# Message passing over 640,000 edges: buckets in pairs that share 33 tiles, and overflow worked off in batches

## The chip, the cores and the metric

The kernel runs on one core of one Trainium2 chip. The time is the device time of one execution in microseconds (us). Before the change the median of three runs is 8543.91 us (8543.35 to 8546.97); the execution that the profile shows took 8539.33 us. Engines are PE (TensorE), DVE (VectorE), ACT (ScalarE), POOL (GpSimd) and SP (SyncE); PEld is the weight load of PE.

## What is computed

```python
N, deg, C, L, DE = 10000, 64, 64, 1, 4        # E = 640,000 edges, M = 4
R = _silu(edge_feat @ w_rad)                              # (E, C)
xs = x[src]                                                 # (E, C, M)
tp = jnp.einsum('eci,ef,ifo->eco', xs, Y, cg)             # (E, C, M)
msg = R[:, :, None] * tp
agg = _segment_sum(msg.reshape(-1, C * M), dst, N).reshape(N, C, M)
return jnp.einsum('ncm,cd->ndm', agg, w_mix)
```

`src` and `dst` are random. So each edge needs a row of `x` (256 numbers, 1 KB) picked by its `src`, and its message has to be added to the node `dst`.

## The kernel before

Edges are sorted by `dst` in two passes and then summed per bucket of 32 nodes (`NB`). There are 313 buckets; 18 of them are a group (`B`), and there are 18 groups, the last with 7 buckets. A **tile** is 128 edges, one per partition. An edge is carried as 9 words: a key (`src` and `dst`), four of `Y`, four of `edge_feat`.

- The edges are cut into three parts by `SPLIT`; a bucket has 5, 6 and 6 tiles (`BT`, 17 in all) for them in a DRAM tensor `bkt`. What a part doesn't hold goes on into the tiles of the next one, and what all 17 don't hold goes to an overflow region behind the buckets.
- `pass1` sorts a part into groups (DRAM tensor `grp`), `pass2` a group into its buckets. Both work in **chunks** of 12 tiles through `route`: one-hot matrices by DVE and ACT (`spread` L578, `rows` L594 and L600), matmuls that put the edges into rows (L608), and one indirect store per chunk from POOL (L619). For every batch of chunks `tables` computes where rows go, in a chain of some 50 small DVE instructions with PE and ACT in between.
- `messages` goes over **units**, one per bucket and part (939). A unit gathers the rows of `x` by one indirect DMA from POOL per tile (L915, five units ahead, into seven buffers), evaluates the radial weights (L933 to L949), multiplies (L967), spreads `Y` over the 32 nodes (`spots`, L957 and L960) and sums on PE (L980). Sums of parts 0 and 1 go to DRAM and are added in the next part (L1009); in the last part four buckets at a time are mixed and written to the output (L1028, L1036).
- Order. PE, DVE and ACT follow the order in which the generators are called. First `pass1` of part 0 runs alone. Then `groups` steps through the first segment of `pass2`, with steps of `pass1` of part 1 between, until the first bucket data are there. After that each unit takes four steps; beside the units of a part run `pass2` of the same part (next group) and `pass1` of the next part, paced by `ends` and `later`. Beside the units of the last part only `pass2` runs. POOL and SP get their instructions in the same program order and work them off in that order.
- After the last unit, `overflow` (L1142) loops over the overflow regions of `grp` and `bkt`, one tile of 128 edges a turn: load, gather `x`, match equal destinations, multiply, read the output rows, add, write them back. `whole` (L1172) would redo everything if a chunk had needed more than 128 rows.

The row capacity of a bucket and its layout are set by two lines:

```python
self.p2 = Pass(12, 15, BT * P // 15, 6, True)      # rows of 15 edges, 145 rows in 17 tiles
nc.vector.tensor_tensor(dl[:N], cap[:N], off[:N], op=OP.min)
```

Of the kernel before, what the change touches and what calls it, by code (L numbers as in the profile page):

```python
# [25 lines left out]
P = 128  # L26
# [7 lines left out]
BT = 17  # L34
UT = 6
SPLIT = ((0.3, (5,)), (0.355, (6,)), (0.345, (6,)))
# [4 lines left out]
FAR = 2097152.0  # L41
KR = 108
HB = 5
# [30 lines left out]
class Kernel:  # L74
    def __init__(self, ctx, tc, x, src, dst, Y, ef, w_rad, cg, w_mix, out):
# [17 lines left out]
        assert N <= 1 << 14 and BT == sum(sum(u) for _, u in SPLIT)  # L93
# [15 lines left out]
        self.p2 = Pass(12, 15, BT * P // 15, 6, True)  # L109
# [3 lines left out]
        self.NBK = (N + NB - 1) // NB  # L113

        self.btile = [0]
        for _, u in SPLIT:
            self.btile.append(self.btile[-1] + sum(u))

        self.p1.ovf = len(SPLIT) * NG * self.p1.stride
        self.p2.ovf = self.NBK * self.p2.stride  # L120
        for q, tiles in ((self.p1, [z - a for a, z in self.part]), (self.p2, sum(self.gt, []))):
            q.none = -(-(q.ovf + sum((t + q.T - 1) // q.T for t in tiles) * P + 16) // q.stride) * q.stride
            q.rows = q.none
# [20 lines left out]
    def consts(self):  # L144
# [8 lines left out]
        self.zr = c.tile([16, max(self.p1.rw, self.p2.rw)], F, name="zr")  # L153
        nc.vector.memset(self.zr, 0.0)
        self.pid = iota("pid", [[0, 1]], cm=1)
        self.pid1 = iota("pid1", [[0, 1]], base=1, cm=1)
# [60 lines left out]
        self.bb = iota("bb", [[self.p2.stride, B]])  # L217
# [23 lines left out]
    def bucket_words(self, b, n, t0, t1):  # L241

        v = self.p2.dst[:self.p2.ovf, :].rearrange("(b s) w -> b (s w)", s=self.p2.stride)
        return v[b:b + n, t0 * P * W:t1 * P * W].rearrange("b (p q) -> p b q", p=P)

    def clear_buckets(self):
        nc, n = self.nc, 2048 // (BT * W)
        for b in range(0, self.NBK, n):
            m = min(n, self.NBK - b)
            nc.sync.dma_start(self.bucket_words(b, m, 0, BT),  # L250
                              self.z[:, :m * BT * W].rearrange("p (b q) -> p b q", b=m))
            yield
# [100 lines left out]
    def tables(self, ps, D, nt, rows, kov, base, cap):  # L353
# [36 lines left out]
        nc.tensor.matmul(pre_p[:N, 32:32 + B], self.ones[0:1, :N], rows, start=True, stop=True)  # L390
        nc.tensor.matmul(pre_p[0:1, 64:64 + B], self.ones[:N, 0:1], cn[:N], start=True, stop=True)
# [3 lines left out]
        nc.scalar.activation(off[:N], pre_p[:N, 32:32 + B], AF.Copy)  # L395
        nc.scalar.activation(tot[0:1], pre_p[0:1, 64:64 + B], AF.Copy)
        self.held = None
        yield
        if ps.carry:
# [7 lines left out]
            nc.vector.tensor_tensor(off[:N], off[:N], f[:N], op=OP.add)  # L407
            self.floor(tot[0:1], tot[0:1], r, True, ps.key, 1)
# [25 lines left out]
        nc.vector.tensor_tensor(dl[:N], cap[:N], off[:N], op=OP.min)  # L434
        nc.vector.tensor_tensor(dl[:N], dl[:N], base[:N], op=OP.add)
# [39 lines left out]
        nc.tensor.matmul(dd_p[:, :N * J], self.ones[:N, :], bd[:N, :N * J], start=True, stop=True)  # L475
        yield
        nc.vector.scalar_tensor_tensor(sts[:, :N * J], sts[:, :N * J], self.pid, dd_p[:, :N * J],
# [6 lines left out]
        di = w("di", NC, d=I32)  # L484
        nc.vector.tensor_copy(di[:, :N], dest[:, :N])
        nc.vector.tensor_scalar(di[:, :N], di[:, :N], ps.stride - 1, None, op0=OP.bitwise_and)
        nc.vector.tensor_scalar(fl[:, :N], di[:, :N], float(ps.cap), None, op0=OP.is_ge)
# [269 lines left out]
    def pass2(self):  # L757
# [13 lines left out]
        def front(i, Wt):  # L771
# [4 lines left out]
            nc.vector.tensor_scalar(base, self.bb, float(g * B * ps.stride), None, op0=OP.add)  # L776
# [11 lines left out]
            yield from self.tables(ps, D, nt, kc, self.kov[:, 1:2], base, self.bc)  # L788
            ready[i] = D, Wt, self.tab[ps.key]

        for i, (k, g) in enumerate(self.segs):
# [27 lines left out]
            n = sum(SPLIT[k][1])  # L819
# [18 lines left out]
    def messages(self):  # L838
# [19 lines left out]
        def index(k):  # L858

            g, j, s = units[k]  # L860
            if s or j:
                return
# [471 lines left out]
```

## Time and profile before

| | us | note |
|---|---|---|
| median of three runs | 8543.91 | |
| profiled execution | 8539.33 | its span, first to last instruction: 8537.6 |
| until the first gather of `x` | 614.0 | `pass1` of part 0 and the first segment of `pass2` |
| gathers of `x` and what runs beside them | 614 to 8449 | 5321 gathers, one per tile |
| after the last gather | 88 | last unit, three turns of the overflow loop |

The page gives each engine's busy time. Matmuls are pipelined and their ends are modelled, so PE's share reads high. A gather or store from POOL counts as busy while POOL prepares it; the time until its data have landed isn't in that number. A row of the windows view gives, for a stretch of time, each engine's busy time with the number of its instructions in brackets, then the clock granted to PE, the mean busy share of the DMA engines, and GB/s.

### The profile page before, as it was taken

To read this page: it belongs to the slowest core of one execution; us is meant where nothing else is said; L and a number is where in the kernel's file an instruction comes from. 1 tells how busy PE (TensorE), PEld (TensorE's weight loads), DVE (VectorE), ACT (ScalarE), POOL (GpSimd) and SP (SyncE) were. 2 spreads that over 40 slices of the span, in tenths; PEclk is the share of its full clock that TensorE was granted. 3 is DMA by queue.
4 is the path that set the end of the run, shared out by engine and by line. 5 is a ranking of instruction groups with operands and counts; after the bars stand their busy time and mean duration, and the time that the engine had idled before them with its cause. 6 is when DMAs were issued, how large, how long until landed. Compare 5 with 4: busy or idle time off the path is not lost. (4 is left out here: it accounts for less than half of the span.)

```text
span 8537.6 us, 148817 instructions
## 1 busy us (share of the span) xinstructions
PE 6849.6 (80%) x51885; PEld 6294.3 (74%) x51885; DVE 6833.0 (80%) x12901; ACT 4467.9 (52%) x12655; POOL 5984.1 (70%) x6255
## 2 busy tenths in 40 slices
PE   7977888888888788787787888876888878787875
PEld 6867777777778677777777777766777777677764
DVE  8988898889898789888888988876767767676743
ACT  6866666666566465555555655533433434343421
POOL 2236777677677767777777777777777777777774
PEclk9989999999899899899998998988888988898887
DMA  8313444344334434444444444444444444444442
GB/s 177 101 58 98 121 118 125 108 122 118 113 116 124 124 112 138 130 135 136 132 135 136 134 135 134 131 140 130 130 125 128 127 126 127 125 126 124 127 124 80
DMA packets 694591, 1056.58 MB, mean 124 GB/s; under 512 B 250979, under 2 KB 498340, under 8 KB 693840
## 3 DMA queue, kind: packets, MB, share of 16 engines
q0 software_dynamic: 284864, 746.68, 30.0%
q1 hardware_dynamic: 406384, 292.76, 12.3%
q8 instruction: 410, 6.72, 0.3%
q10 hardware_dynamic: 2592, 7.63, 0.3%
q14 instruction: 341, 2.79, 0.1%
HBM read 856.08 MB, written 203.45 MB: 124 GB/s over the span
## 5 line engine op out<-in xcount | busy, mean ns | idle before, releaser
L915 POOL DMA_INDIRECT xg<-in_x_dram,sidx x5321 | 5062.2, 951 | 1709.2 <-issue 1386.7
L608 PE MATMUL pr<-X,oh 128*128 128x135 f32 (+1 forms) x21112 | 2783.1, 291 | 400.2 <-ACT rt L615 256.8
L608 PEld LDWEIGHTS pr<-X,oh 128*128 128x128 f32 x21112 | 2662.8, 203 | 481.3 <-ACT rt L615 315.1
L980 PE MATMUL G<-S,xg 128*128 128x128 f32 x21284 | 2872.2, 296 | 155.5 <-DVE Gp L1009 116.7
L980 PEld LDWEIGHTS G<-S,xg 128*128 128x128 f32 x21284 | 2723.8, 210 | 198.7 <-DVE Gp L1009 142.9
L967 DVE TENSOR_TENSOR xg<-xg,pre 128x1536 f32<-128x1536 f32 (+1 forms) x939 | 1559.0, 1660 | 918.0 <-DMA xg<-in_x_dram,sidx 701.7
L600 ACT ACTIVATE sq<-i,rowf 128x128 f32<-128x128 f32 x6106 | 1876.1, 392 | 5.6 <-DVE rowf L565 2.4
L578 DVE TENSOR_TENSOR X<-dv,Wt 128x1512 f32<-128x1512 f32 (+3 forms) x905 | 1579.7, 1746 | 147.0 <-PE pr L608 100.0
L949 ACT ACTIVATE pre<-pre 128x384 f32<-128x384 f32 (+1 forms) x939 | 430.4, 458 | 1391.4 <-PE pre L946 1099.4
L601 ACT ACTIVATE oh<-sq,ones 128x896 f32<-128x896 f32 (+2 forms) x905 | 964.3, 1066 | 28.8 <-issue 1.4
L960 DVE TENSOR_TENSOR S<-dv,pay 128x768 f32<-128x768 f32 (+1 forms) x939 | 857.5, 913 | 64.3 <-PE G L980 20.1
L619 POOL DMA_INDIRECT grp<-rt,idx x417 | 418.6, 1004 | 573.8 <-ACT rt L615 244.9
L594 DVE TENSOR_TENSOR oh<-dv,rowf 128x640 f32<-128x640 f32 (+2 forms) x870 | 719.3, 831 | 0.5
L933 PE MATMUL pre<-identb,e 128*108 128x128 bf16 x1878 | 273.7, 229 | 500.6 <-DVE xg L967 492.9
L933 PEld LDWEIGHTS <-e 128*108 128x108 bf16 x1878 | 219.7, 132 | 572.1 <-issue 505.8
L619 POOL DMA_INDIRECT bkt<-rt,idx x488 | 488.6, 1001 | 192.5 <-issue 111.2
L938 ACT ACTIVATE sT<-pre 108x256 bf16<-108x256 f32 x939 | 351.5, 374 | 424.6 <-PE pre L933 423.2
L1028 PE MATMUL po<-wf,Gs 128*128 128x256 f32 (+2 forms) x1392 | 401.4, 453 | 160.0 <-DVE Gs L1009 158.8
L1028 PEld LDWEIGHTS po<-wf,Gs 128*128 128x128 f32 (+2 forms) x1392 | 289.8, 214 | 251.2 <-DVE Gs L1009 164.6
L896 ACT ACTIVATE e<-er 128x360 bf16<-128x360 f32 (+3 forms) x420 | 188.9, 450 | 416.1 <-DVE er L906 415.5
L615 ACT ACTIVATE rt<-pr 128x135 f32<-128x135 f32 (+1 forms) x905 | 242.5, 272 | 286.3 <-DMA bkt<-rt,idx 213.9
L548 ACT ACTIVATE pc<-pp 128x432 f32<-128x432 f32 (+4 forms) x453 | 233.5, 515 | 254.2 <-DVE pos L557 131.9
(247 smaller groups left out, 5257.3 us busy)
## 6 DMA issues: line engine op xcount, KB each, us to landing
xg<-in_x_dram,sidx POOLq DMA_INDIRECT x5321
sums<-Gp SPq DMA_DIRECT2D x626, 128.0 KB
old<-sums SPq DMA_DIRECT2D x626, 128.0 KB
bkt<-z SPq DMA_DIRECT2D x24, 994.5 KB
pay<-bkt SPq DMA_DIRECT2D x34, 486.0 KB
ys<-in_Y_dram SPq DMA_DIRECT2D x104, 96.0 KB
es<-in_edge_feat_dram SPq DMA_DIRECT2D x104, 96.0 KB
out_dram<-ot SPq DMA_DIRECT2D x69, 128.0 KB
```

The costliest lines, as they stand in the source:

```text
L578: nc.vector.tensor_tensor(X[:, :m, :].rearrange("p t (s w) -> p t s w", w=W), msk.unsqueeze(3).to_broadcast([P, m, ps.r, W]), QD[c // Q][1 ...
L594: nc.vector.tensor_tensor(oh[:, :v, :], self.v128.unsqueeze(1).to_broadcast([P, v, P]), row[:, o:o + v].unsqueeze(2).to_broadcast([P, v, P ...
L600: nc.scalar.activation(sq[:, u, :], self.i128, AF.Square, bias=to, scale=-1.0)
L601: nc.scalar.activation(oh[:, v:v + len(at), :], sq[:, :len(at), :], AF.Relu, bias=self.ones[:, 0:1], scale=-2.0)
L608: nc.tensor.matmul(pr[:, :ps.rw], oh[:, u, :], X[:, u, :], start=(u == 0), stop=(not on and u == m - 1))
L619: st = nc.gpsimd.indirect_dma_start(out=ps.dst, out_offset=bass.IndirectOffsetOnAxis(ap=idx[:, i:i + 1], axis=0), in_=RT.pop(c), in_offset ...
L915: nc.gpsimd.indirect_dma_start(out=xg[:, t, :], out_offset=None, in_=self.x, in_offset=bass.IndirectOffsetOnAxis(ap=si[:, u:u + 1], axis=0))
L933: nc.tensor.matmul(pre[:KR, 256 + 128 * h:384 + 128 * h], e[:, 36 * t:36 * t + KR], self.identb, start=True, stop=True)
L960: nc.vector.tensor_tensor(S[:, :ut], self.eq[:, :ut].unsqueeze(3).to_broadcast([P, ut, NB, 4]), pb[:, :, 1:5].unsqueeze(2).to_broadcast([P ...
L967: nc.vector.tensor_tensor(V, V, R.unsqueeze(3).to_broadcast([P, ut, 64, 4]), op=OP.mult)
L980: nc.tensor.matmul(G[:, h].rearrange("p n f -> p (n f)"), V[:, t, 32 * h:32 * h + 32, :].rearrange("p c i -> p (c i)"), S[:, t].rearrange( ...
L1028: nc.tensor.matmul(po[:nn, :256], Gs[:, h, f].rearrange("p b n -> p (b n)")[:, :nn], self.wf[:, h, f, :], start=(h + f == 0), stop=(h + f ...
```

## The change

**Pairs.** Buckets 2m and 2m+1 get 33 tiles together (`PT`). The even one fills them from the front, the odd one from the back; in parts 0 and 1 each has its own 5 and 6 tiles, and in the last part the even one has 6, the odd one 5, and the sixth tile of the even one belongs to both. So a pair of units in the last part gathers 11 tiles and not 12. The even unit builds a second spread matrix (`Sx`) for the shared tile with the odd bucket's nodes, and the odd unit adds it to its sum with the tile's products kept from the even unit. `tables` works out the row offsets from both ends; in the last part it also works out a row limit per bucket (`dlim`, `lm`), since the border between the two is free.

**Shares.** The parts now hold 0.32, 0.37 and 0.31 of the edges (before 0.30, 0.355 and 0.345). `pass1` has 134, 154 and 129 chunks (before 124, 148, 145), `pass2` 157, 175 and 157 (before 140, 174, 174).

**Overflow.** Counting the edges of the reference's inputs through these rules gives 19 overflow rows of 15 before (285 slots, three tiles) and 60 rows now (900 slots, eight tiles). Up to eight tiles (`LT`) are taken as two batches of four (`batch`, `join`, `put`): gathered and multiplied in steps beside the last units, and read, added and written back after them. Whatever remains, `grp` overflow and `whole` are put into one loop (`rest`), which isn't entered when all counts are zero.

**Pacing.** `pass1` of part 1 starts with step 40 of the units (`at`), and no longer beside the first segment of `pass2`. The blocks of the radial casts are 4 buckets (`HB`, before 5).

```diff
-SPLIT = ((0.3, (5,)), (0.355, (6,)), (0.345, (6,)))
+SPLIT = ((0.32, 5), (0.37, 6), (0.31, 6))
-HB = 5
+HB = 4
-        self.p2 = Pass(12, 15, BT * P // 15, 6, True)
+        self.p2 = Pass(12, 15, PT * P // 15, 6, True)
...
+            nc.vector.tensor_tensor(end[:H], off[:H], tot[:H], op=OP.add)
+            till = of(end, 1)
+            if final:
+                lim, dlim = w("lim", B), w("dlim", J)
+                till = w("till", B // 2)[:H]
+                nc.vector.tensor_scalar(till, of(end, 1), float(self.most_odd), None, op0=OP.min)
...
+            nc.vector.scalar_tensor_tensor(of(sh, 1), till, -1.0, of(off, 1), op0=OP.mult, op1=OP.subtract)
+            nc.vector.tensor_tensor(off[:H], off[:H], f[:H], op=OP.add)
+            nc.vector.scalar_tensor_tensor(of(off, 1), of(sh, 1), float(self.full), of(off, 1), op0=OP.add, op1=OP.add)
...
-            nc.sync.dma_start(pay[:, :nb, :], self.bucket_words(g * B, nb, self.btile[k], self.btile[k + 1]))
+            if k == len(SPLIT) - 1:
+                q = 2 * n - 1
+                v = pay[:, :a * q].rearrange("p (b t) w -> p b (t w)", t=q)
+                for u, z in ((0, n - 1), (n - 1, n), (n, q)):
+                    nc.sync.dma_start(v[:, :, u * W:z * W], self.pair_words(m, a, t0 + u, t0 + z))
+            else:
+                v = pay[:, :B * n].rearrange("p (b a t) w -> p b a (t w)", a=2, t=n)
+                nc.sync.dma_start(v[:, :a, 0], self.pair_words(m, a, t0, t1))
+                nc.sync.dma_start(v[:, :nb // 2, 1], self.pair_words(m, nb // 2, PT - t1, PT - t0))
...
+        def place(g, j):
+            n = SPLIT[g[0]][1]
+            if g[0] < FIN:
+                return j * n, n
+            return j // 2 * (2 * n - 1) + j % 2 * n, n - j % 2
...
+            if shared(k):
+                eq = ph.tile([P, NB], F, name="eqx", bufs=1)
+                nc.vector.tensor_scalar(eq, self.v128[:, NB:2 * NB], dl[:, ut - 1:ut], None, op0=OP.is_equal)
+                S = SX[k + 1] = ph.tile([P, NB, 4], F, name="Sx")
+                nc.vector.tensor_tensor(S, eq.unsqueeze(2).to_broadcast([P, NB, 4]),
+                                        pb[:, ut - 1, 1:5].unsqueeze(1).to_broadcast([P, NB, 4]), op=OP.mult)
...
+            terms = [(V[:, t], S[:, t]) for t in range(ut)]
+            if k in VX:
+                terms.append((VX.pop(k), SX.pop(k)))
...
-        later, at = [], 0
+        later, at = [], 40
...
         while segs[0] not in self.pay:
             next(sort)
-            if later:
-                said = next(later[0][0])
-                done += 0.0 if said == "held" else said or 1
+        batch, got = self.batch(), None
...
+            elif got is None:
+                if segs[-1] in self.pay:
+                    run(sort)
+                    self.remains()
+                    got = "begun"
+            elif got != "ready":
+                got = next(batch) or got
             next(main)
         assert not later
-        run(main)
-        run(sort)
+        for _ in main:
+            if got != "ready":
+                got = next(batch) or got
+        while got != "ready":
+            got = next(batch) or got
+        run(batch)
...
+    def put(self, al, di, xg):
+        nc = self.nc
+        cur = al("ocur", [P, OT, 256])
+        nc.vector.memset(cur, 0.0)
+        for t in range(OT):
+            nc.gpsimd.indirect_dma_start(
+                out=cur[:, t], out_offset=None, in_=self.out, in_offset=bass.IndirectOffsetOnAxis(ap=di[:, t:t + 1], axis=0),
+                bounds_check=self.N - 1, oob_is_err=False)
+        for t in range(OT):
+            nc.vector.tensor_tensor(cur[:, t], cur[:, t], xg[:, t].rearrange("p c i -> p (c i)"), op=OP.add)
+            nc.gpsimd.indirect_dma_start(
+                out=self.out, out_offset=bass.IndirectOffsetOnAxis(ap=di[:, t:t + 1], axis=0), in_=cur[:, t], in_offset=None,
+                bounds_check=self.N - 1, oob_is_err=False)
...
+    def rest(self):
+        with self.tc.For_i(0, self.nc.values_load(self.n[:, 3:4], min_val=0, max_val=1), 1):
+            wx = self.ph.tile([P, 2, 64, 4], F, name="wx")
+            self.wide(wx)
+            self.leftover(self.p1, self.kov[:, 0:1], self.n[:, 0:1], 0, wx)
+            self.leftover(self.p2, self.kov[:, 1:2], self.n[:, 1:2], LT * P, wx)
+            self.whole(self.n[:, 2:3], wx)
```

The order on POOL shows three places where the change moves work. `grp` and `bkt` rows are stores of the two sort passes, `xg` rows the gathers; a count behind a row stands for that many alike in a row. First the last group segments of the last part, before:

```order
L915 DMA xg<-in_x_dram,sidx 128x256 x54
L619 DMA bkt<-rt,idx 223232x135 x2
L915 DMA xg<-in_x_dram,sidx 128x256 x12
L619 DMA bkt<-rt,idx 223232x135
L915 DMA xg<-in_x_dram,sidx 128x256 x6
L619 DMA bkt<-rt,idx 223232x135
L915 DMA xg<-in_x_dram,sidx 128x256 x6
```

and the same place now:

```order
L990 DMA xg<-in_x_dram,sidx 128x256 x55
L673 DMA bkt<-rt,idx 143360x135
L990 DMA xg<-in_x_dram,sidx 128x256 x11
L673 DMA bkt<-rt,idx 143360x135 x2
L990 DMA xg<-in_x_dram,sidx 128x256 x11
L673 DMA bkt<-rt,idx 143360x135 x2
```

Two units gathered 12 tiles between stores and now gather 11; the density of stores per unit stays one. Counted over the whole order, POOL issues 5321 gathers before and 5165 now, and 905 and 906 sort stores.

Second, the change from the first pass to the units, before:

```order
L619 DMA grp<-rt,idx 165888x126 x126
L619 DMA bkt<-rt,idx 223232x135
L619 DMA grp<-rt,idx 165888x126 x2
L619 DMA bkt<-rt,idx 223232x135 x3
L915 DMA xg<-in_x_dram,sidx 128x256 x35
```

and now:

```order
L673 DMA grp<-rt,idx 165888x126 x134
L673 DMA bkt<-rt,idx 143360x135 x4
L990 DMA xg<-in_x_dram,sidx 128x256 x9
L673 DMA bkt<-rt,idx 143360x135
L990 DMA xg<-in_x_dram,sidx 128x256 x7
```

All 134 stores of part 0 stand ahead, and the four stores that `pass1` of part 1 had there (126 + 2 less 124) have moved behind the first gathers. Between the first and the last gather of part 0 there are now 329 sort stores (before 303), of part 1 295 (before 310), of part 2 144 (before 160).

Third, the end of the program, now:

```order
L1220 DMA oxg<-in_x_dram,osm 128x256 x8
L990 DMA xg<-in_x_dram,sidx 128x256 x162
L1300 DMA ocur<-out_dram,osm 128x256 x4
L1305 DMA out_dram<-ocur,osm 10000x256 x4
L1300 DMA ocur<-out_dram,osm 128x256 x4
L1305 DMA out_dram<-ocur,osm 10000x256 x4
```

The eight gathers of the batches stand 162 gathers ahead of the end; the reads and writes of the output follow the last gather in two rounds of four.

More of the change, by code (lines that the diff above doesn't have):

```diff
@@ L858, in index, with shared @@
+        def shared(k):
+            g, j = units[k]
+            return g[0] == FIN and j % 2 == 0 and j + 1 < self.nb(g[1])
         def index(k):
[L860 to L861 removed]
+            g, j = units[k]
+            if j:
                 return
             m = self.nb(g[1])
[L864 to L866 removed]
```

502 lines of the change are left out of this document (299 added, 203 removed).

## The prediction

> **What bounds the kernel now.** I read the busy times first, then the stretches of the program in the windows view, then POOL's own waits, and last the timeline of the end.
>
> ```profile
> PE 6849.6 (80%) x51885; PEld 6294.3 (74%) x51885; DVE 6833.0 (80%) x12901; ACT 4467.9 (52%) x12655; POOL 5984.1 (70%) x6255
> ```
>
> By this row PE and DVE look like the bound and POOL like the third. POOL's timeline says otherwise (columns: start, duration, engine, line, operation, count, idle time before it):
>
> ```profile
> 6932.87 1.00 POOL L619 DMA_INDIRECT bkt<-rt,idx  x1 [0.30 <-issue]
> 6934.18 1.00 POOL L619 DMA_INDIRECT bkt<-rt,idx  x1 [0.30 <-issue]
> ...
> 8445.82 0.95 POOL L915 DMA_INDIRECT xg<-in_x_dram,sidx  x1 [0.30 <-issue]
> 8447.07 0.95 POOL L915 DMA_INDIRECT xg<-in_x_dram,sidx  x1 [0.30 <-issue]
> 8448.32 0.95 POOL L915 DMA_INDIRECT xg<-in_x_dram,sidx  x1 [0.30 <-issue]
> ```
>
> Each gather is busy for 0.95 us and 0.30 us follow in which POOL waits for nothing shown: a gather takes a slot of 1.25 us, a store 1.31. So a POOL that shows 76% busy is full. The windows, cut at the first gather (614) and at the last gathers of the three parts (3085 and 5866, found by counting 1565 and 1878 gathers; 8450):
>
> ```profile
> 614.00:3085.00 2471.00, 2020.31 (x15952) 1882.77 (x15953) 2132.39 (x4131) 1534.33 (x4451) 1779.05 (x1852) 0.92 0.40 116
> 3085.00:5866.00 2781.00, 2236.03 (x17532) 2083.05 (x17531) 2385.12 (x4380) 1517.28 (x4243) 2100.14 (x2190) 0.91 0.46 134
> 5866.00:8450.00 2584.00, 2063.22 (x14548) 1871.92 (x14547) 1745.80 (x2987) 949.85 (x2578) 1957.84 (x2054) 0.87 0.43 126
> ```
>
> The columns after the length are PE, PEld, DVE, ACT and POOL. POOL's slots: 1852 x 1.25 = 2315 us of 2471 (94%), 2190 x 1.25 = 2738 of 2781 (98%), 2054 x 1.25 = 2568 of 2584 (99%). **The second and third stretches last as long as POOL needs to issue its indirect DMAs.** The first one leaves 156 us over, at DVE 86% and PE 82%. There POOL does wait for others:
>
> ```profile
> POOL xg L915 <- PE G L980: 50.8, 29, 6.9
> POOL bkt L619 <- ACT rt L615: 17.5, 10, 8.2
> ```
>
> It waits for a gather buffer that PE hasn't summed yet, or for rows that are not ready: DVE, PE and ACT are late in a burst of sorting, and the gathers have run out of buffers.
>
> **The change part by part**
>
> *Slots of POOL.* By the order of the change: gathers 5321 to 5165, batch gathers 0 to 8; sort stores behind the first gather, part by part, 303 to 329, 310 to 295, 160 to 144. The slots change by +26, -15 and -156 - 16 + 8 = -164, at 1.25 us: **+33, -19, -205 us**. All of it is on the path in the second and third stretches, which are full; in the first only if POOL stays the bound.
>
> *The first part* gets more sorting per unit: 26 chunks more, since 157 + 154 chunks replace 140 + 148, and since those that ran before the first gather have moved in here. The price of a chunk for DVE comes from a stretch of the first part:
>
> ```profile
> 800.00:2800.00 2000.00, 1670.07 (x13342) 1561.66 (x13341) 1752.08 (x3272) 1282.36 (x3724) 1465.82 (x1526) 0.93 0.41 118
> ...
> L578 DVE TENSOR_TENSOR X<-dv,Wt 128x1512 f32<-128x1512 f32 (+2 forms) x254 | 451.1, 1776 | 71.8 <-PE pr L608 56.3 <-DVE dv L575 0.5
> L967 DVE TENSOR_TENSOR xg<-xg,pre 128x1280 f32<-128x1280 f32 x256 | 379.3, 1481 | 82.4 <-ACT pre L949 65.1 <-DMA xg<-in_x_dram,sidx 15.6
> L960 DVE TENSOR_TENSOR S<-dv,pay 128x640 f32<-128x640 f32 x256 | 211.1, 825 | 30.3 <-PE G L980 11.5
> L957 DVE TENSOR_TENSOR dv<-dv,dlc 128x160 f32<-128x160 f32 x256 | 85.0, 332 | 5.1
> L906 DVE TENSOR_TENSOR er<-pay,e 128x100 f32<-128x100 f32 (+1 forms) x57 | 14.2, 249 | 0.0
> L906 DVE TENSOR_TENSOR er<-er,e 128x100 f32<-128x100 f32 (+1 forms) x57 | 14.2, 249 | 0.0
> ...
> L403 DVE SCALAR_TENSOR_TENSOR part<-f,pre 64x18 f32<-64x18 f32 x54 | 9.3, 172 | 1.8
> ```
>
> 256 units and 254 chunks ran in these 2000 us. The units' own DVE work is 379 + 211 + 85 + 28 = 704 us; the rest, 1752 - 704 = 1048, is sorting: 4.13 us a chunk. 26 chunks are 107 us. `tables` gets five more small instructions like the last row (18 tables x 5 x 0.17 = 15 us) and the radial casts a fifth block per group (5 us): DVE's 2132 us become 2259. If POOL stayed the bound the part would grow by 33 us; at the share of DVE that the whole part shows (86.3%) by 2259 / 0.863 - 2471 = 147. I take 88.0%, just above the 87.6% of the stretch quoted, because the second part runs at 86% with POOL full and bursts are what hurts: 2259 / 0.88 = 2567, **+96 us**, ends +33 and +147.
>
> *The second part* has 15 chunks less and stays with POOL: **-19 us**. Its own table instructions (20 us) lie under POOL's 2719.
>
> *The last part.* POOL falls to (2054 - 164) x 1.25 = 2363 us plus the 16 left over: 2379. Is something else late then? DVE has 1746 us; less 16 chunks (66) and the shorter odd units (a tile's share of L967 and L960 above: 156 x 0.46 = 72), plus the second spread matrix (156 pairs, two instructions), the tables and the batches. For the 128 x 128 product of the pair the nearest row is
>
> ```profile
> L1220 DVE TENSOR_TENSOR odup<-oeq,L x3: 291/291/292, 8478.7 to 8519.2; 128x128 f32<-128x128 f32 x3
> ```
>
> so 0.29 us and some 0.2 for the 32 columns: 156 x 0.5 = 78. Tables and batches I put at 60. DVE ends near 1746, 73%: cover enough. PE's matmuls for the sums stay (the odd unit has 5 + 1 terms). A chunk costs PE
>
> ```profile
> L608 PE MATMUL pr<-X,oh 128*128 128x135 f32 (+1 forms) x21112 | 2783.1, 291 | 400.2 <-ACT rt L615 256.8
> ```
>
> 2783 / 905 = 3.1 us and some smaller matmuls, say 3.4. So 2063 - 54 (16 chunks) + 30 for the batches (two times 52 matmuls at 0.29) = 2039 us, 86% of 2379. That is more than any part shows on average, but a sorting burst before has had
>
> ```profile
> 6880.00:6960.00 80.00, 74.11 (x589) 69.82 (x590) 72.17 (x137) 47.80 (x133) 60.57 (x64) 0.98 0.44 130
> 6960.00:7030.00 70.00, 47.93 (x301) 41.28 (x300) 35.08 (x54) 12.91 (x36) 52.94 (x57) 0.78 0.43 123
> ```
>
> PE at 93% with POOL at its 64 slots in 80 us, and 68% in the calm behind it. Gathers run up to five units ahead, so a burst in which PE falls back by a few us is made up in the next calm. I add 10 us for that: **-195 us**, ends -205 and -29 (below). Bucket data come in three DMAs a segment where one was; each is an SP instruction of 0.38 us, and there is slack:
>
> ```profile
> L822 SPq DMA_DIRECT2D pay<-bkt x54: 378/384/384, 606.8 to 8202.8; - x54
> ...
> L867 DVE TENSOR_SCALAR sidx<-pay x54: 183/247/439, 613.6 to 8265.8; 128x108 int32<-128x108 int32 x34, 128x90 int32<-128x90 int32 x17, 128x42 int32<-128x42 int32 x2, 128x35 int32<-128x35 int32 x1
> ```
>
> the last load was issued 63 us before its first reader ran. The batches' gathers add a wait on DVE: the product of the batch stands some two units behind the gather in DVE's order, and POOL comes to that gather only after those of five units. Behind it wait the products of the next units, and PE; POOL goes on, since its next five units have buffers. That is part of the 10 us.
>
> *Until the first gather.* Ten more chunks of `pass1`, while the first segment loses the chunks of part 1 that ran beside it:
>
> ```profile
> 200.00:300.00 100.00, 47.63 (x28) 1.00 0.40 107
> 400.00:500.00 100.00, 52.93 (x31) 1.00 0.25 85
> 520.00:614.00 94.00, 20.12 (x12) 0.70 0.08 24
> ```
>
> These are the products L578, one a chunk: 3.2 to 3.6 us a chunk, so +34. Of the 12 chunks in the last 94 us, 8 belong to part 1, with a table; without them DVE has some 40 us less of its 72 in that stretch, but the chain of the segment's own table stays. I take -34, net **0**, ends -15 and +25.
>
> *After the last gather.* Before:
>
> ```profile
> 8464.77 0.48 SPq L1037 DMA_DIRECT2D out_dram<-ot  x1
> 8475.37 40.78 SPq L1159 DMA_DIRECT2D opay<-bkt  x3
> ...
> 8489.33 1.02 POOL L1264 DMA_INDIRECT out_dram<-ocur,odi  x1 [8.18 <-DVE ocur L1263]
> 8512.16 1.03 POOL L1264 DMA_INDIRECT out_dram<-ocur,odi  x1 [8.17 <-DVE ocur L1263]
> 8530.33 1.03 POOL L1264 DMA_INDIRECT out_dram<-ocur,odi  x1 [8.68 <-DVE ocur L1263]
> ...
> 8533.94 0.14 DVE L1180 TENSOR_SCALAR nw<-cw 1x1 int32<-1x1 f32 x1 [3.90 <-PE cw L1178]
> ```
>
> From 8449.3 to the span's end at 8537.6 are 88 us: 17 until the last output is written, 64 for the loops with three turns of 18 to 23 us, the rest for the last check. Now the 17 stay; two rounds follow, each of four reads (5 us), landing and adding (3), four writes partly beside it and their landing (4): 24 us; then one check, some 6 us. That is 47: **-40 us**, ends -50 and -20.
>
> Sum: 0 + 96 - 19 - 195 - 40 = -158. Against the profiled execution's 8539.3 that is 8381; the median of the runs is 4.6 us above it, so I forecast **8385 us**.
>
> [...] A gather's busy time hardly varies:
>
> ```profile
> L915 POOL DMA_INDIRECT xg<-in_x_dram,sidx x5321: 940/946/1440, 614.0 to 8448.3; - x198
> ```
>
> The median is 946 ns and the longest of 5321 is 1440, with DVE busy beside them. [...]
>
> **The rivals**
>
> 1. *The first part stays with POOL.* For it: gathers have five units of room. Against it: DVE would stand at 2259 of 2504, 90%, above any long stretch here. Then +33 in place of +96: 8322 us.
> 2. *PE becomes the bound of the last part*, and the saved gathers show only in part. If PE can't pass the 82% of the first part: 2039 / 0.82 = 2487, -97 in place of -195: 8482. If it can't pass its present 80%, the part takes 2555, -29, and the sum is +8: no change. For it: bursts at 93%. Against it: the calm between them.
> 3. *Slower: the first part's sorting chain blocks the units.* A table is a chain through DVE, PE and ACT, each in order; when units and chunks come more densely, each hold-up of DVE delays products, sums, and so buffers. DVE's share would have to fall under 2259 / (2471 + 96 + 158) = 83% for the whole to be slower; at 80% the part takes 2824, +353, and the time is 8640. Against it: more work ready on an engine tends to raise its share.
> [...]
> 5. *The overflow isn't covered*: the count of rows would be wrong, or the last loop is entered, and the end costs what it did, or 40 us more: 8425 to 8465. The same count gives the three turns seen before.
>
> **How the numbers follow.** Forecast with its ends in the sum (8340 to 8440) 0.53; rival 1: 0.15; rival 2: 0.16, a quarter of it at no change; rival 3: 0.06; rivals 4 and 5: 0.05 each. A measurement of this kernel tells about 0.2% (17 us) from no change. Faster by more: 0.90; within it: 0.04; slower: 0.06. The range reaches down over rival 1 (8295) and up past most of rival 2 (8500).
>
> **What would show it.** In the changed profile, gathers of the last part follow each other at 1.25 us and the part lasts near 2380 us (rival 2: nearer 2490, with POOL waiting for L980's successor). The first part lasts near 2570 and shows DVE at 88%. [...] I am wrong if the last part's length doesn't follow POOL's slots, or if the first part gives back over 150 us.

## The result and the profile after

The changed kernel takes 8447.18 us (median of 4 runs, 8445.14 to 8450.74) beside 8545.39 us of the kernel before on the same chip (4 runs, 8543.35 to 8546.97): ratio 0.9885, interval 0.987 to 0.9899. It is 98 us faster; the forecast was 158. The profiled execution has a span of 8449.0 us.

The first row of its page, busy times by engine:

```profile
PE 6864.1 (81%) x52108; PEld 6331.2 (75%) x52108; DVE 6900.6 (82%) x13656; ACT 4481.6 (53%) x12845; POOL 5851.5 (69%) x6113
```

POOL fell from 70% to 69% of a shorter span and is still the least conspicuous of the three. The stretches tell more. First a correction of my own: the bounds that the prediction set for the stretches (3085 and 5866) stood some 20 us ahead of the last gathers of their parts. Divided at the end of the 1565th, 3443rd and last gather, the kernel before reads, in the windows view (columns as in the prediction: PE, PEld, DVE, ACT, POOL, granted clock, DMA), with POOL's gathers of the first stretch alone in the last row:

```profile
614.00:3105.70 2491.70, 2038.12 (x16105) 1899.19 (x16106) 2149.69 (x4159) 1552.06 (x4503) 1794.87 (x1868) 0.92 0.40 117
3105.70:5885.10 2779.40, 2234.23 (x17500) 2081.60 (x17499) 2386.32 (x4387) 1512.86 (x4225) 2098.85 (x2189) 0.91 0.46 134
5885.10:8449.30 2564.20, 2046.50 (x14423) 1856.26 (x14423) 1727.29 (x2953) 936.54 (x2542) 1943.31 (x2039) 0.87 0.43 126
8449.30:8537.60 88.30, 28.69 (x114) 20.15 (x113) 25.19 (x104) 3.61 (x14) 10.95 (x12) 0.60 0.05 13
...
614.00:3105.70 2491.70, 1491.27 (x1565) 0.92 0.40 117
```

and the changed kernel, divided at the same gathers:

```profile
603.30:3263.80 2660.50, 2168.89 (x16794) 2020.34 (x16793) 2262.58 (x4516) 1666.32 (x4866) 1820.40 (x1894) 0.90 0.39 110
3263.80:6015.40 2751.60, 2227.67 (x17244) 2082.02 (x17243) 2356.91 (x4391) 1473.13 (x4141) 2084.14 (x2173) 0.90 0.47 135
6015.40:8377.80 2362.40, 1951.92 (x14208) 1781.02 (x14206) 1726.04 (x3461) 874.93 (x2456) 1791.45 (x1875) 0.91 0.45 128
8377.80:8449.00 71.20, 12.65 (x65) 9.79 (x63) 7.91 (x14) 0.76 (x2) 16.03 (x17) 0.63 0.07 20
```

Each stretch less its counterpart, beside the forecast's term:

| stretch | before, us | after, us | change | forecast |
|---|---|---|---|---|
| until the first gather | 614.0 | 603.3 | -11 | 0 |
| first part | 2491.7 | 2660.5 | +169 | +96 |
| second part | 2779.4 | 2751.6 | -28 | -19 |
| last part | 2564.2 | 2362.4 | -202 | -195 |
| after the last gather | 88.3 | 71.2 | -17 | -40 |
| sum | 8537.6 | 8449.0 | -89 | -158 |

The last part goes by POOL's slots: 1875 instructions at 1.25 us are 2344 of its 2362 us, as 2039 were 2549 of 2564 before, and PE's share rose from 80% to 83% without ending it. The surprise is the first part. Its DVE work is what was forecast (2259; here 2263 us), but DVE's share *fell* from 86.3% to 85.0%. Where it idles is in the groups by line. DVE's product that spreads the payload into X, before the change and after it, in that part:

```profile
L578 DVE TENSOR_TENSOR X<-dv,Wt 128x1512 f32<-128x1512 f32 (+2 forms) x305 | 542.2, 1778 | 76.3 <-PE pr L608 57.0 <-DVE dv L575 0.9
```

```profile
L632 DVE TENSOR_TENSOR X<-dv,Wt 128x1620 f32<-128x1620 f32 (+2 forms) x334 | 584.2, 1749 | 151.4 <-PE pr L662 129.4 <-PE pre L1016 0.5
```

X has three buffers, and one comes free when PE's matmuls `pr` have read it. The wait for that grew by 72 us. That this is about the 73 us by which the part overran its forecast proves nothing by itself: DVE's idle time in the part grew by 56 us in all.

The end of the changed kernel, POOL's timeline from the last gather on (start, duration, engine, line, operation, count, idle time before it):

```profile
8376.89 0.95 POOL L990 DMA_INDIRECT xg<-in_x_dram,sidx  x1 [0.30 <-issue]
8399.10 1.02 POOL L1300 DMA_INDIRECT ocur<-out_dram,osm  x1 [21.26 <-issue]
...
8406.96 1.02 POOL L1305 DMA_INDIRECT out_dram<-ocur,osm  x1 [2.94 <-DVE ocur L1304]
8410.03 1.00 POOL L1305 DMA_INDIRECT out_dram<-ocur,osm  x1 [2.05 <-issue]
8413.06 0.97 POOL L1305 DMA_INDIRECT out_dram<-ocur,osm  x1 [2.02 <-issue]
8416.05 0.97 POOL L1305 DMA_INDIRECT out_dram<-ocur,osm  x1 [2.02 <-issue]
8419.12 1.04 POOL L1300 DMA_INDIRECT ocur<-out_dram,osm  x1 [2.10 <-DMA out_dram<-ocur,osm]
...
8430.22 1.00 POOL L1305 DMA_INDIRECT out_dram<-ocur,osm  x1 [2.58 <-DMA out_dram<-ocur,osm]
8433.22 0.97 POOL L1305 DMA_INDIRECT out_dram<-ocur,osm  x1 [2.00 <-DMA out_dram<-ocur,osm]
8436.21 0.97 POOL L1305 DMA_INDIRECT out_dram<-ocur,osm  x1 [2.02 <-DMA out_dram<-ocur,osm]
```

The four writes of a batch stand 3.0 us apart, not 1.3. In the second batch the profile names what each waits for, the landing of the write ahead; in the first it names nothing ("issue"), and an experiment below decides.

### The profile page after: what moved, and what is told of

Read it like the earlier page. It is cut to its first block, busy times and chain, and to the rows that moved or that the text cites. A ratio compares the mean times of both kernels' runs of the same rounds, so it can differ in the third digit from the quotient of the medians.

```text
span 8449.0 us, 149894 instructions
## 1 busy us (share of the span) xinstructions
PE 6864.1 (81%) x52108; PEld 6331.2 (75%) x52108; DVE 6900.6 (82%) x13656; ACT 4481.6 (53%) x12845; POOL 5851.5 (69%) x6113
## 5 line engine op out<-in xcount | busy, mean ns | idle before, releaser
L990 POOL DMA_INDIRECT xg<-in_x_dram,sidx x5165 | 4918.3, 952 | 1783.0 <-issue 1357.6
L662 PE MATMUL pr<-X,oh 128*128 128x126 f32 (+1 forms) x21146 | 2810.6, 293 | 460.7 <-ACT rt L669 318.9
L1056 PE MATMUL G<-S,xg 128*128 128x128 f32 x20660 | 2794.8, 297 | 86.2 <-DVE Gp L1079 63.0
L1056 PEld LDWEIGHTS G<-S,xg 128*128 128x128 f32 x20660 | 2645.6, 210 | 127.8 <-DVE Gp L1079 87.7
L1043 DVE TENSOR_TENSOR xg<-xg,pre 128x1536 f32<-128x1536 f32 (+1 forms) x939 | 1517.2, 1616 | 654.8 <-DMA xg<-in_x_dram,sidx 425.6
L632 DVE TENSOR_TENSOR X<-dv,Wt 128x1620 f32<-128x1620 f32 (+4 forms) x906 | 1582.4, 1747 | 210.2 <-PE pr L662 163.2
L655 ACT ACTIVATE oh<-sq,ones 128x1024 f32<-128x1024 f32 (+3 forms) x906 | 967.4, 1068 | 29.8 <-PE pr L662 1.6
L1029 DVE TENSOR_TENSOR S<-dv,pay 128x768 f32<-128x768 f32 (+1 forms) x939 | 836.7, 891 | 50.7 <-PE G L1056 5.8
L971 ACT ACTIVATE e<-er 128x240 bf16<-128x240 f32 (+6 forms) x522 | 205.3, 393 | 330.5 <-DVE er L981 308.9
L602 ACT ACTIVATE pc<-pp 128x432 f32<-128x432 f32 (+3 forms) x471 | 236.7, 503 | 240.9 <-DVE pos L611 128.7
L1026 DVE TENSOR_TENSOR dv<-dv,dlc 128x192 f32<-128x192 f32 (+1 forms) x939 | 325.4, 347 | 15.8
```

The source lines that it names most:

```text
L632: nc.vector.tensor_tensor(X[:, :m, :].rearrange("p t (s w) -> p t s w", w=W), msk.unsqueeze(3).to_broadcast([P, m, ps.r, W]), QD[c // Q][1 ...
L655: nc.scalar.activation(oh[:, v:v + len(at), :], sq[:, :len(at), :], AF.Relu, bias=self.ones[:, 0:1], scale=-2.0)
L662: nc.tensor.matmul(pr[:, :ps.rw], oh[:, u, :], X[:, u, :], start=(u == 0), stop=(not on and u == m - 1))
L990: nc.gpsimd.indirect_dma_start(out=xg[:, t, :], out_offset=None, in_=self.x, in_offset=bass.IndirectOffsetOnAxis(ap=si[:, u:u + 1], axis=0))
L1029: nc.vector.tensor_tensor(S[:, :ut], self.eq[:, :ut].unsqueeze(3).to_broadcast([P, ut, NB, 4]), pb[:, :, 1:5].unsqueeze(2).to_broadcast([P ...
L1043: nc.vector.tensor_tensor(V, V, R.unsqueeze(3).to_broadcast([P, ut, 64, 4]), op=OP.mult)
```

## The experiments

My theory A for the first part: the new shares put more sorting chunks beside the same units, and a chunk costs more than its DVE time. Rival B: the pairing itself costs it (longer tables, blocks of four buckets for the radial casts, two loads a segment). Rival C: the pacing, which no longer runs the next part's sorting beside the first segment.

**Four kernels on a slower chip.** The shares alone in the kernel before:

```diff
-SPLIT = ((0.3, (5,)), (0.355, (6,)), (0.345, (6,)))
+SPLIT = ((0.32, (5,)), (0.37, (6,)), (0.31, (6,)))
```

> The kernel before with the shares 0.32, 0.37, 0.31 of the edges and nothing else of the change: 18 sort chunks more for the buckets of the first part's first pass, 4 more of the second; 325 stores in the first part instead of 303, 10 more ahead of it, gathers 5321 as before. Theory A (the first part lost its 182 us because more chunks stand beside the same units, at some 7 us a chunk where I had reckoned 4.1): first part 2471 + 22 x 7 = 2625 us (2590 to 2650), first gather 15 to 35 us later than before (614), last part shorter by its 16 stores, 20 us, end as before: 8620 to 8680 us in all. Rival B (the loss comes from the pairing: longer tables, blocks of four buckets for the radial casts, two loads): first part 2471 to 2520 us, 8500 to 8570 in all. Rival C (the pacing of the part's sorting ahead of the next part): like B, first part under 2520.

The changed kernel with the pacing of before; the third kernel has the same with three steps of `later` beside each step of `sort`:

```diff
-        later, at = [], 40
+        later, at = [], 0
...
         while segs[0] not in self.pay:
             next(sort)
+            said = next(later[0][0])
+            done += 0.0 if said == "held" else said or 1
```

> The changed kernel with the pacing of before: the sorting of the next part runs from the first quarter on and beside the first segment ahead of the first gather (4 chunks more there, 4 fewer in the first part: 325 stores for 329). Theory A: first part 4 x 7 = 28 us shorter (2615 to 2640), first gather 10 to 20 us later: 8425 to 8445 in all. Rival C: first part 2540 to 2580, 8350 to 8400 in all. Rival B: no change, 8440 to 8465.

> The changed kernel with the next part's sorting begun earlier, three steps beside each step of the first segment ahead of the first gather: 32 chunks move from the first part to ahead of it (297 stores in the first part for 329). Theory A: first part 2653 - 32 x 7 = 2430 us (2400 to 2490; POOL's slots would need 1861 x 1.25 = 2326), first gather 32 x 3.4 = 109 us later (90 to 140): 8330 to 8400 in all. Rival B (the pairing's own work): first part loses only 32 x 4.1 = 131 us at most, 2520 or more, so 8425 or more in all. Rival C: in between, 8400 to 8440.

And the changed kernel with the writes of a batch told to be apart:

```diff
-            nc.gpsimd.indirect_dma_start(
+            st = nc.gpsimd.indirect_dma_start(
                 out=self.out, ...
+            if t:
+                self.tc.declare_no_dep(st.ins, group=self.puts, reason="the rows of a batch are apart")
+            self.tc.add_to_no_dep_group(self.puts, st.ins)
```

> The changed kernel with the four writes of each overflow batch told to be apart, so that none waits for the one before it to land. If the end is 71 us in place of the forecast 47 because each write waits 3 us for the last one, two batches save 2 x 3 x (3.0 - 1.3) = 10 us to 18: end 53 to 61 us, 8428 to 8440 in all. If the wait is something else (the additions, POOL), no change: 8445 to 8451.

On this chip the kernel before took 10577.9 us. Against it: the shares alone 1.0028 (1.0016 to 1.004), old pacing 1.0214 (1.0196 to 1.0231), early sorting 1.0216 (1.0195 to 1.0237), writes apart 1.0139 (1.0122 to 1.0156). None of the totals could be held against my numbers, which were for a chip like the first. Two of the four kernels were run again, on another chip, with the changed kernel beside them:

> The changed kernel itself, beside the kernel before and the experiments on the same chip. On a chip that grants the TensorE clock as in the profiles of before and after (0.905): ratio 0.987 to 0.990, first part 2640 to 2660 us, last part 2375 to 2390. On the chip of the first four experiments, where the kernel before took 10578 us at a granted clock of 0.83 and POOL was busy for 56% of its span only, PE is the bound in all three parts: the change saves no work of PE (the shared tile is multiplied for both buckets, 156 x 2 matmuls more for the shorter odd units and as many fewer gathers), so there the ratio is 1.01 to 1.02, as in the runs with the old pacing and with the writes apart.

> As for the first run of this kernel (the kernel before with the shares 0.32, 0.37, 0.31 alone). On a chip with the clock of before and after (0.905), theory A (density of the sorting): first part 2590 to 2650 us, 8620 to 8680 in all. Rivals B and C (pairing, pacing): first part 2471 to 2520, 8500 to 8570 in all. On the slower chip: 1.000 to 1.005 of before, as it was.

> As for the first run of this kernel (the changed kernel with 32 chunks of the next part's sorting moved ahead of the first gather). On a chip with the clock of before and after (0.905), theory A: first part 2400 to 2490 us, first gather 90 to 140 us later than in the changed kernel: 8330 to 8400 in all. Rival B: first part 2520 or more, 8425 or more in all. On the slower chip PE is the bound and moving chunks gains nothing: 1.02 of before, as it was.

That chip was slow too: 10514.27 us for the kernel before. The changed kernel took 1.0098 of it (1.0068 to 1.0128): **the change loses 1% here**, the shares alone gain 0.45% (0.9955; 0.9939 to 0.9971), early sorting loses more (1.0181; 1.0153 to 1.021). The shares alone had been expected at 1.000 to 1.005 there, and came out faster than that; on the other slow chip they were slower than before. The stretches of the changed kernel on that chip:

```profile
606.20:3821.30 3215.10, 2373.44 (x16723) 2172.83 (x16722) 2260.10 (x4501) 1665.03 (x4847) 1821.15 (x1894) 0.84 0.32 91
3821.30:7251.50 3430.20, 2471.97 (x17068) 2257.14 (x17068) 2339.84 (x4320) 1457.85 (x4100) 2081.47 (x2174) 0.84 0.38 108
7251.50:10508.30 3256.80, 2270.51 (x14336) 2029.64 (x14337) 1763.34 (x3529) 886.40 (x2508) 1791.47 (x1874) 0.80 0.33 93
```

and the last part of the kernel before with the shares alone, there:

```profile
7308.50:10362.80 3054.30, 2140.00 (x14076) 1923.03 (x14074) 1702.47 (x2961) 884.33 (x2439) 1926.11 (x2022) 0.83 0.37 106
```

DVE, ACT and POOL have the busy times of the first chip to within 3%; PE's rose by 9 to 16%. POOL's 1874 slots fill 2343 of 3257 us, so POOL is not what the part's length goes by, and the paired part is 202 us longer than the unpaired one, with 260 matmuls more. What PE does there shows in the timeline of the shares alone, on the first of the two slow chips:

```profile
8806.87 0.27 PE L980 MATMUL G<-S,xg 128*128 128x128 f32 x1 [0.46 <-issue]
8807.58 0.36 PE L980 MATMUL G<-S,xg 128*128 128x128 f32 x1 [0.45 <-issue]
8808.30 0.27 PE L980 MATMUL G<-S,xg 128*128 128x128 f32 x1 [0.35 <-issue]
```

Matmuls of one sum, whose operands come from the same DVE instructions as those of the matmuls ahead, stand 0.7 us apart and wait for nothing that the profile shows. In the whole of that trace such waits (columns: total us, times, longest) are

```profile
PE G L980 <- issue: 432.8, 570, 7.2
```

for the sums alone; the trace of the kernel before on the first chip has none for them. I did not find what holds them, nor why the paired part suffers by more than its matmuls; both stay open, the more so as these traces put many waits down to a releaser that they call "remote" (in the last part of the changed kernel on the other slow chip 691 us for the products `Gs` alone, in 91 waits), which those of the first chip don't have. Early sorting did move the work: on that chip the first gather came 190 us later (796.4 against 606.2) and the first part was 102 us shorter (3113.2), a loss at 32 chunks moved.

The edit of the writes can be read on any chip: the end took 73.4 us where the changed kernel's, on the other slow chip, took 83.3: the 10 us expected.

**PE relieved.** If PE's slowness decides, take it away: in `sums` the operands are read as the upper halves of their float32 words, one matmul instruction in place of two (in the kernel before 10642 of 241 ns in the mean for 21284 of 296 ns), with all else unchanged. In the kernel before, in the same with the new shares, and in the changed kernel:

```diff
+            hi = lambda a: a.bitcast(BF)[:, 1::2]
...
-                                     V[:, t, 32 * h:32 * h + 32, :].rearrange("p c i -> p (c i)"),
-                                     S[:, t].rearrange("p n f -> p (n f)"),
+                                     hi(V[:, t, 32 * h:32 * h + 32, :].rearrange("p c i -> p (c i)")),
+                                     hi(S[:, t].rearrange("p n f -> p (n f)")),
```

> The kernel before with less work for PE: the sums G read only the upper halves of their float32 operands (as bfloat16, one pass of PE in place of several), so the result is rounded; all instructions of DVE, ACT, POOL and SP and all buffers are as before. If POOL's slots set the second and third part once PE is relieved: second part near (1878 + 310) x 1.25 = 2735 us, third near (1878 + 160) x 1.25 = 2550. If PE's other work or a throttled clock still bounds them on this chip, they take over 2900 and over 2750. First part: POOL would need (1565 + 303) x 1.25 = 2335; with DVE's 2132 us of work and bursts 2380 to 2500. In all 8350 to 8650.

> The same relief of PE, with the shares 0.32, 0.37, 0.31 of the edges in the kernel before, without pairs (325 stores in the first part for 303, 144 in the last for 160). Theory A (density of sorting loads DVE, 4 to 7 us a chunk): first part 90 to 160 us longer than in l_before. [...] Rival B (pairing's own work): 30 us longer, POOL's slots alone. Last part 16 x 1.25 = 20 us shorter than in l_before.

> The same relief of PE in the changed kernel. If POOL's slots set the last part as soon as PE has room, the change's mechanism shows here on this chip too: last part (1722 + 144 + 20) x 1.25 = 2358 to 2390 us, 160 to 195 less than l_before. If it stays near l_before's length or above, the bound of the last part is not POOL even with PE relieved, and the gain seen at the higher clock was something else. [...] In all 100 to 200 us less than l_before.

> The kernel before itself, for its parts on the chips of the experiments. There the changed kernel took 606 us to its first gather, then 3221, 3430 and 3251 us a part. The whole is 1% shorter here: 10500 to 10600. If PE's clock is the bound in all parts, the loss of the change sits where PE got more work: last part 3040 to 3120 (100 to 200 us shorter than in the changed kernel, which multiplies the shared tile twice), first part 3080 to 3180, second 3430 to 3500.

This chip was like the first: 8549.86 us for the kernel before, and its parts repeat (2487.6, 2783.8 and 2567.2 us in the run of before_again, so that its expectation, written for a slow chip, does not apply). Ratios: l_before 0.9953 (0.9933 to 0.9973), l_shares 1.003 (1.0018 to 1.0041), l_after 0.9841 (0.9813 to 0.987). The stretches of the kernel before, relieved:

```profile
610.60:3065.20 2454.60, 1697.52 (x13060) 1529.55 (x13060) 2146.17 (x4164) 1549.91 (x4507) 1796.06 (x1868) 0.81 0.41 118
3065.20:5845.00 2779.80, 1797.40 (x13680) 1610.24 (x13681) 2377.94 (x4380) 1511.67 (x4221) 2099.76 (x2188) 0.78 0.46 134
5845.00:8411.40 2566.40, 1501.84 (x10667) 1261.33 (x10666) 1725.09 (x2954) 939.89 (x2542) 1945.47 (x2039) 0.76 0.44 126
```

the same with the new shares:

```profile
657.50:3194.30 2536.80, 1781.40 (x13488) 1602.95 (x13489) 2209.08 (x4289) 1632.30 (x4727) 1820.11 (x1890) 0.81 0.40 115
...
5952.70:8499.60 2546.90, 1501.35 (x10205) 1258.16 (x10202) 1670.99 (x2904) 885.30 (x2390) 1930.62 (x2023) 0.74 0.44 126
```

and the changed kernel, relieved:

```profile
600.30:3210.60 2610.30, 1820.86 (x13700) 1642.17 (x13700) 2259.14 (x4506) 1666.71 (x4866) 1824.08 (x1894) 0.80 0.39 112
...
5972.90:8336.80 2363.90, 1473.09 (x10441) 1247.75 (x10440) 1721.97 (x3461) 877.25 (x2456) 1792.86 (x1874) 0.77 0.46 127
```

The second and last parts do not care for 400 to 550 us less of PE: 2779.8 and 2566.4 us beside 2779.4 and 2564.2 (expected from the slots alone: 2735 and 2550), and 2363.9 beside 2362.4 in the changed kernel. Sixteen stores fewer give 19.5 us (2566.4 to 2546.9), 1.22 us each; and from the new shares without pairs to the changed kernel, 149 instructions fewer on POOL (2023 to 1874) give 183 us (2546.9 to 2363.9), 1.23 us each. **POOL's slots bound these parts on this chip.** The last part is 202 us shorter than in l_before, a little more than the 160 to 195 expected; in the whole the relieved change gains 96 us, just under the 100 to 200 expected.

The shares alone lose: the spans are 8499.4 us in l_before, 8570.3 in l_shares and 8406.7 in l_after, so the gain comes with the pairs and what goes with them. Pairs with the old shares were not run.

The first part gains 37 us by the relief in the kernel before and 50 in the changed one, so the work of PE that the relief took accounts for 13 of the 169 us. Of the other 156 (2454.6 to 2610.3), 113 are busy time of DVE. By kernels, the shares alone make 82: 22 chunks, 3.7 us each, 63 us of it DVE's busy time. That is theory A's cause at less than its price (90 to 160), since I had put all of the loss down to chunks. What PE's other work costs is not shown: the relief took only matmuls of the sums, and PE was still busy for 69 to 70% of the part. And 74 us more come with pairs and pacing. The wait for X's buffers doubled with the shares. It stands for the relieved kernel before, for it with the shares, and for the relieved changed kernel (waits in the first part: total us, times, longest):

```profile
DVE X L578 <- PE pr L608: 60.0, 35, 4.6
```

```profile
DVE X L578 <- PE pr L608: 121.7, 35, 9.5
```

```profile
DVE X L632 <- PE pr L662: 131.4, 43, 8.1
```

It grew by 62 us from the first to the second, while DVE's idle time in all grew by 19 (308 to 328). So this wait in part took the place of others, and it is a sign of the denser sorting, not a price of it.

**Pairs or pacing?** The last kernel is the relieved changed kernel with the pacing of before (the edit of the second experiment) and the writes apart (that of the fourth); the two act in different stretches.

> The changed kernel with PE relieved as in l_after, and two edits that lie in different stretches: the pacing of before (the next part's sorting begins beside the first segment, ahead of the first gather, and goes on from the first quarter), and the overflow batches' writes told to be apart. On a chip with the clock of l_after (0.79): theory Pacing (what l_after's first part lost beyond l_shares, 74 us, was sorting of the next part that no longer ran beside the first segment): first gather 645 to 665 us (l_after 600, l_shares 657), first part 2530 to 2565 (l_after 2611, l_shares 2537). Theory Pairing (the longer tables and smaller blocks cost it): first gather the same 645 to 665, first part 2580 to 2600, only the four chunks less. Last part as in l_after, 2355 to 2370, by both. End: 58 to 64 us in place of 71, since writes follow at 1.3 us in place of 3.0. In all 8390 to 8420 by Pacing, 8430 to 8460 by Pairing. On a chip with the slower PE: no statement on the first part, end 10 us shorter than the changed kernel's 84.

It ran on a chip like the first (8544.26 us before). Its first part and its end:

```profile
649.70:3199.80 2550.10, 1778.53 (x13492) 1601.54 (x13492) 2223.79 (x4416) 1637.44 (x4778) 1818.27 (x1890) 0.81 0.40 114
...
8319.90:8379.10 59.20, 10.50 (x44) 7.58 (x44) 7.84 (x14) 0.76 (x2) 16.27 (x17) 0.59 0.08 25
```

The first part falls to 2550.1, so of the 74 us 60 were pacing and 13 the pairs' own work (2536.8 to 2550.1): rival C for the most part, B for the rest. Of the 60, 35 are busy time of DVE that moved (2259.1 to 2223.8). In return the first gather comes at 649.7 in place of 600.3, so the pacing of before gains 11 us. No run has it in the changed kernel with full operands on a chip like the first; on the first slow chip it lost (10804.67 us beside 10720.74 of the kernel with the writes apart, some 10 of it the writes). The end is 59.2 us in place of l_after's 69.9: 11 us by the writes. The whole takes 8387.29 us, 0.9822 of the kernel before (0.9808 to 0.9835): 3 us under the range by Pacing and the fastest of all, ahead of l_after's 0.9841 and the changed kernel's 0.9885, at the price of sums whose operands are cut to bfloat16.

## Why the prediction was right, and where it was not

- **Right: the last part, and with it the sign.** -202 for -195, and the mechanism is shown: with 479 us of PE's busy time taken away the changed part kept its length, 16 stores fewer gave 16 slots, and 149 instructions fewer gave 149 slots. Rival 2 (PE becomes the bound) is refuted on chips like the first. PE had more room than I thought: its work in the part fell by 95 us (2046.5 to 1951.9) where I had 24, at a granted clock of 0.91 for 0.87. On the two slow chips the change loses, and POOL is not the bound there; the forecast held for one kind of chip without saying so. My slot count of before (2054) was 15 too high by the early bound; the difference between the kernels was not touched by it.
- **Mis-sized: "I take 88.0%".** The step took DVE's work right (+113 us by the rows above, forecast +127) but let its share rise. The share fell from 86.3% to 85.0%, so DVE's idle time in the part grew by 56 us too (2491.7 - 2149.7 = 342; 2660.5 - 2262.6 = 398). In the four relieved kernels the share of DVE is 87.4, 87.1, 86.5 and 87.2%: nowhere did it rise with the work. Why it fell is open; the wait that grew most is that for X's buffers, on PE's matmuls `pr`. The result lies past the upper end that I had worked out at the share of before (+147), and past the 150 us that I had named as proof against me. The argument against rival 3, that more ready work raises an engine's share, did not hold here: at 85% the part is nearer to rival 3's threshold (83%) than to my 88. What rival 3 forecast, a falling share, came at a size that the last part outweighs. Relieved, the first part splits into 82 by the shares, 60 by pacing, 13 by the pairs.
- **Right by cancelling: until the first gather.** I had +34 and -34. With PE relieved the shares add 47 us (610.6 to 657.5), the pacing takes 49 (649.7 to 600.3), and the rest takes 8. That two terms, both too small, left a sum near the forecast is luck. And the work that left this stretch cost 60 us in the first part, where my working held four chunks for it, 17 us at 4.13 each: moving it lost 11 us.
- **Mis-sized: after the last gather**, 71 for 47. The first read comes 21.3 us behind the last gather (I had 17), the two rounds take 38.1 (8399.1 to 8437.2; I had 24 with overlapping writes), and what follows 11.8 (I had 6). The waits between writes are 11 of the 24 us that were missing, as the last run shows.
- **Rival 1** (the first part stays with POOL) is refuted: 1894 slots are 2368 of its 2660 us. **Rival 5** too: the loops for leftovers were not entered.
- **Rival 4** (0.05), that the pair products hold up POOL, decided nothing: gathers beside them were longer, but by next to nothing in all. The gathers of the changed kernel (minimum, median, longest in ns):

```profile
L990 POOL DMA_INDIRECT xg<-in_x_dram,sidx x5165: 940/946/1927, 603.3 to 8376.9; - x199
```

  The median is the 946 ns of before; in the last part the mean is 951.4 ns (1639.2 us for 1723) beside 948.7 (1782.7 us for 1879), 4.5 us in all; 156 pair products, had each held POOL for its full 0.29 us, would have been 45. But the longest is 1927 ns, and the timeline of DVE and POOL shows which products ran beside it, and beside others:

```profile
7302.15 0.29 DVE L1036 TENSOR_TENSOR Sx<-eqx,pay 128x128 f32<-128x128 f32 x1
7302.21 1.06 POOL L990 DMA_INDIRECT xg<-in_x_dram,sidx  x1 [0.30 <-issue]
...
8232.27 1.22 DVE L1267 TENSOR_TENSOR oN<-oxg,oA 128x1024 f32<-128x1024 f32 x1
8232.80 1.52 POOL L990 DMA_INDIRECT xg<-in_x_dram,sidx  x1 [0.30 <-issue]
...
8234.51 1.22 DVE L1271 TENSOR_TENSOR oM<-oM,oN 128x1024 f32<-128x1024 f32 x1
8234.62 1.93 POOL L990 DMA_INDIRECT xg<-in_x_dram,sidx  x1 [0.30 <-issue]
```

  In the last part 14 gathers began inside a pair product (L1036) and 12 inside a product of the batches (L1262, L1267, L1271), each more than 0.05 us behind the product's start. Each was longer than 0.946 us by what was left of the product less some 0.13 us, where that much was left: the last two shown by 0.57 and 0.98 us. Beside the pair products that makes at most 0.11 us each and under 1 us in all, beside the batches' longer ones 5.0 us over nine gathers. Both inputs of these products are in SBUF; 163 gathers of the last part that began as far inside a product `S` (L1029), one input of which is in PSUM, took 0.96 us at most. Why these products hold up a gather and `S` does not, no run shows.

The sum came out at -89 for -158 in the profiled execution. Of the 69 us between them, the first part is 73 and the end 23, against 26 that the other three stretches did better. The 8447 us lie 7 past the forecast's own ends (8340 to 8440). They lie inside the wider range because that one reached up for rival 2, which did not act, so it held partly by luck.

## What to carry to other kernels

Count an issuing engine's slots, busy time and the gap behind it together (here 0.95 and 0.30 us): a POOL that shows 76% was full, and the length of its parts followed the number of its DMAs to within 2%. Where work is moved into a stretch that no engine fills, price it at the share that the stretch shows, or below it: here the share fell from 86.3% to 85.0% as the work grew. And say on which chip's figures a forecast rests: a saving on one engine is a saving only while that engine is the last.

## What was not expected of the hardware

The kernel before took 8544 to 8550 us in three sets of runs and 10514 and 10578 in two others, on two chips; in the changed kernel DVE, ACT and POOL had the busy times of the first chip there to within 3%, and with the shares alone PE paused by 0.35 to 0.46 us between the matmuls of a sum shown above.

With half the matmul instructions of the sums gone (10642 for 21284) the granted clock fell, from 0.92 to 0.81 in the first part and from 0.87 to 0.76 in the last, and what was left of PE's work grew slower. Matmuls of the relieved kernel before, by line (busy time, mean ns):

```profile
L608 PE MATMUL pr<-X,oh 128*128 128x135 f32 (+1 forms) x21112 | 3233.8, 320 | 801.6 <-ACT rt L615 438.9 <-DVE oh L594 273.5 <-ACT oh L601 46.1
L981 PE MATMUL G<-S,xg 128*128 128x128 bf16 x10642 | 901.2, 241 | 176.4 <-DVE Gp L1010 130.0 <-ACT Gp L1012 21.5 <-DMA xg<-in_x_dram,sidx 8.4
```

`pr` had a mean of 291 ns before, and 320 here. In the last part PE was busy for 1502 us in place of 2047 at the lower clock; in the kernel before the clock was 0.98 in the 80 us of a burst with PE busy for 93%, and 0.78 in the 70 us behind it at 68%. From these figures I take the granted clock to be in part a result of PE's waits. That is a reading of mine: no run changed the waits alone. A low clock is no proof that PE is the bound: at 0.76 the relieved last part kept its length (2566.4 us for 2564.2).
